# Copying the output/denominator bank of a sliding-window attention out of PSUM before the softmax is normalised

## The chip, the cores and the metric

The kernel runs on one core of one Trainium2 chip. The metric is device time in microseconds (us). The engines are PE (matmul; PEld is its weight load), DVE (VectorE), ACT (ScalarE), POOL (GpSimd) and SP (which issues DMAs).

## The reference

Two layers. Each is a sliding-window attention with a residual, then an MLP over the token axis with a residual, on x of shape 1 x 2048 x 512.

```python
def _A_ref(x, wqkv, wo):                      # 32 heads of 16, window of 256 tokens
    qkv = ((x @ wqkv).reshape(B, S, 3, H, Dh)).transpose(2, 0, 3, 1, 4)
    scores = einsum("bhqd,bhkd->bhqk", q, k) * Dh ** -0.5     # masked to 0 <= i - j < 256
    o = einsum("bhqk,bhkd->bhqd", softmax(scores), v)
    return o.transpose(0, 2, 1, 3).reshape(B, S, D) @ wo
def _B_ref(x, w1, b1, w2, b2):                # mixes tokens: w1 is 2048 x 1792, w2 1792 x 2048
    u = gelu(einsum("bsd,sf->bdf", layernorm(x), w1) + b1)
    return (einsum("bdf,fs->bds", u, w2) + b2).transpose(0, 2, 1)
# ... twice: x = x + A(layernorm(x)); x = x + B(layernorm(x))
```

## The kernel before

The kernel describes its work as operations with reads, writes and a cost in nanoseconds. A list scheduler in the kernel gives every operation a time, and with it a fixed place in its engine's queue; the chip then follows that order with semaphores. The scheduler also hands out buffers: an operation whose buffer is not free yet is placed later. So a scarce buffer shows in the order of an engine, not only in waits.

This kernel's matmuls write PSUM, of which it allots eight banks (`PS`, 128 x 8 x 512 in fp32); SBUF is its working memory. Three pairs of banks hold scores. The other two are one pool, shared by "od" (at most one bank: output and denominators of a head group, columns 0-255 and 256-511) and "f", the fillers: QKV, output projection and MLP matmuls that fit between the attention's matmuls.

```python
NPT = 6
pt = sb("pt", [P, NPT, 4, 512])                    # exp buffers, in bf16; w2 blocks borrow them too
rl = sb("rl", [P, 2, 2, 256], dt.float32)
psum2 = Pool("psum2", 3)                           # three pairs of banks for scores
psum = Pool("psum", 2)
psum.classes = {"od": [0, 1], "f": [0, 2]}         # [in use, at most]
# ... attention, for one head group o: 8 heads on 4 x 32 partitions, 256 tokens (64 groups over both layers)
prev_sc[0] = op("tensor", f_sc, ...)               # L614: scores into two pairs of banks
op("scalar", ... ACTF.Exp ...)                     # L628: exp of 128x1024 into pt, two for each set of scores
op("vector", f_mask, ...)                          # L638, L640: mask multiply in pt
op("tensor", f_pv, ... writes=[od[o]] ...)         # L654: p @ v and p @ ones into the od bank
# ... after the last PV of the group:
t, tr = od[o], Tile(p_rl)
op("scalar", lambda e: e.activation(rl[:, tr.slot, 0, :], bank(t)[:, 256:512], ACTF.Ln), ...)        # L671
op("scalar", lambda e: e.activation(rl[:, tr.slot, 1, :], rl[:, tr.slot, 0, :], ACTF.Exp, scale=-1.0), ...)  # L673
op("vector", lambda e: e.tensor_tensor(oT[:, to.slot, o, :], bank(t)[:, 0:256], rl[:, tr.slot, 1, :],
                                       op=ALU.mult), reads=[t, (tr, 1)], ...)                        # L676
```

The od bank is free again when L676 has read it: after an ln, an exp and a product on two engines. The MLP's first product is cut in two. Its first half (L738 before, L740 after the change) needs only the first eight token tiles, so it may fill gaps late in the attention. Its second half (L752, later L754) starts when the attention has ended. L778 (later L780) is the MLP's second product, and L685 (later L687) the output projection.

The softmax here doesn't subtract the row's maximum and nothing guards it: scores larger than these inputs give would overflow.

Of the kernel before, what the change touches and what calls it, by code (L numbers as in the profile page):

```python
# [6 lines left out]
dt = mybir.dt  # L7
ALU = mybir.AluOpType
ACTF = mybir.ActivationFunctionType

P = 128
# [282 lines left out]
def dve_cost(n, mult=1.0, psum=False, ptrs=0):  # L294
    return ((62 if psum else 66) + n * mult) / 0.96 + 60 * ptrs


def act_cost(n, ptrs=0, psum=True):
    return ((61 if psum else 112) + n) / 1.2 + 93 * ptrs
# [29 lines left out]
def bass_interleave_layers__sliding_block__mixer_token_mlp__prompt_kernel(  # L329
# [16 lines left out]
    NFT = F // P  # L346
    EPS = 1e-5
    SMSCALE = 0.25
    NPT = 6

    es = ExitStack()
    with es:
        sb = lambda name, shape, d=dt.bfloat16: es.enter_context(nc.sbuf_tensor(name, shape, d))
# [7 lines left out]
        kbd = sb("kbd", [P, 3, 4, 8, 2, 64])  # L361
        vbd = sb("vbd", [P, 3, 8, 16, 32])
        pt = sb("pt", [P, NPT, 4, 512])
        rl = sb("rl", [P, 2, 2, 256], dt.float32)
        oT = sb("oT", [P, 3, 4, 256])
        uT = sb("uT", [P, NFT, 512])
        w1b = sb("w1b", [P, 4, NT // 2, 256])
# [17 lines left out]
        op = g.op  # L385
# [4 lines left out]
        psum = Pool("psum", 2)  # L390
        psum.classes = {"od": [0, 1], "f": [0, 2]}
        p_xhT, p_qT, p_stg = Pool("xhT", 2), Pool("qT", 2), Pool("stg", 6)
        p_kv, p_pt, p_rl, p_oT = Pool("kv", 3), Pool("pt", NPT), Pool("rl", 2), Pool("oT", 3)
        p_w1 = Pool("w1", 4)


# [18 lines left out]
        def load_w(i):  # L415
# [9 lines left out]
           cost=2600, prio=-1e6)  # L425
# [3 lines left out]
           cost=500, prio=-1e6)  # L429
        op("sync", lambda e: dma_nc(e, bst[:, NFT:], B_b2.rearrange("(t p) -> p t", p=P)), writes=["b2s"], dma=True,  # L430
           cost=500, prio=-1e6)
# [4 lines left out]
        for h in range(2):  # L436
# [5 lines left out]
               reads=["ident"], writes=[("half", h)])  # L442
# [8 lines left out]
           reads=["tri"] + HALF, writes=["ld0"])  # L451
        op("vector", lambda e: e.scalar_tensor_tensor(ldm[:, 0, :], tri[:, 64:128], half[:, 1:2], ldm[:, 0, :],
                                                      op0=ALU.mult, op1=ALU.add), reads=["tri", "ld0"] + HALF,
           writes=["ld0"])
# [27 lines left out]
        def bank(t):  # L482
            return PS[:, 2 * t.slot if t.pool is psum2 else 6 + t.slot, :]
# [107 lines left out]
        def attention(c, tqs, tks):  # L591
            tq, qc = tqs[c // 2], 4 * (c % 2)
            blk = lambda j: (tks[(4 * c + j) // 8], (4 * c + j) % 8)
            plan = attention_plan(c == 0)
            nb = len(plan)
            half = plan[-1][2] * 64
            to = Tile(p_oT)
            for o2 in range(0, 4, 2):

                order = [[(k, o2, 0)] for k in range(nb - 1)] + [[(nb - 1, o2, 0), (nb - 1, o2 + 1, half)]] + \  # L600
                        [[(k, o2 + 1, 0)] for k in range(nb - 1)]
                od = {}
                left = {o2: nb, o2 + 1: nb}
                for su in order:
                    tp, tA, tB = Tile(p_pt), Tile(psum2), Tile(psum2)
                    cols = max(base + plan[k][2] * 64 for k, _, base in su)

                    def f_sc(e, su=su, tt=(tA, tB)):
                        last = None
                        for k, o, base in su:  # L610
                            for j, q0, n, c0 in plan[k][0]:
                                tk, jj = blk(j)
                                for r in range(4):
                                    last = e.matmul(  # L614
                                        PS[:, 2 * tt[r // 2].slot + r % 2, base + c0 * 64:base + (c0 + n) * 64],
                                        lhsT=kbd[32 * r:32 * r + 32, tk.slot, o, jj, :, :].rearrange("p h n -> p (h n)"),
                                        rhs=qT[32 * r:32 * r + 32, tq.slot, o, (qc + q0) * 64:(qc + q0 + n) * 64],
                                        start=True, stop=True, tile_position=(32 * r, 0), skip_group_check=True)
                        return last
                    rd = []  # L620
                    for k, o, _ in su:
                        rd.append((tq, o))
                        for tk in {id(blk(j)[0]): blk(j)[0] for j, _, _, _ in plan[k][0]}.values():
                            rd += [(tk, "k", o, h) for h in range(2)]
                    prev_sc[0] = op("tensor", f_sc, reads=rd, writes=[tA, tB], cost=cols / 2.4 + 15,
                                    prio=len(g.ops), after=[prev_sc[0]] if prev_sc[0] else [], cfg="sc", cls="sc")
                    for i, ts in enumerate((tA, tB)):
                        op("scalar", lambda e, ts=ts, tp=tp, i=i, cols=cols: e.activation(  # L628
                            pt[:, tp.slot, 2 * i:2 * i + 2, 0:cols], PS[:, 2 * ts.slot:2 * ts.slot + 2, 0:cols],
                            ACTF.Exp, scale=SMSCALE), reads=[ts, "acttab"], writes=[(tp, i)], cost=act_cost(2 * cols))  # L630
                    keys = [(tp, 0), (tp, 1)]
                    n = len(su)
                    for c0, nc_, w0 in plan[su[0][0]][1]:
                        def f_mask(e, tp=tp, n=n, c0=c0, w=nc_ * 64, w0=w0):
                            v = pt[:, tp.slot, :, c0 * 64:c0 * 64 + w]
                            msk = ldm[:].rearrange("p a b -> p (a b)")[:, w0 * 64:w0 * 64 + w]
                            if n == 1:
                                return e.tensor_tensor(v, v, msk.unsqueeze(1).to_broadcast([P, 4, w]), op=ALU.mult)  # L638
                            v = stepped(v, n, half)
                            return e.tensor_tensor(v, v, msk.unsqueeze(1).unsqueeze(1).to_broadcast([P, 4, n, w]),  # L640
                                                   op=ALU.mult)
                        op("vector", f_mask, reads=keys + LD, writes=keys, cost=dve_cost(4 * n * nc_ * 64, 0.5))
                    for k, o, base in su:
                        first = o not in od
                        if first:
                            od[o] = Tile(psum, 1, "od")

                        def f_pv(e, k=k, o=o, base=base, tp=tp, first=first, t=od[o]):
                            last, st = None, first
                            for j, q0, n, c0 in plan[k][0]:  # L650
                                tk, jj = blk(j)
                                for den in (0, 1):
                                    for r in range(4):
                                        last = e.matmul(  # L654
                                            bank(t)[32 * r:32 * r + 32, den * 256 + q0 * 64:den * 256 + (q0 + n) * 64],
                                            lhsT=onesbd[:] if den else vbd[:, tk.slot, jj, 4 * o + r, :],
                                            rhs=pt[:, tp.slot, r, base + c0 * 64:base + (c0 + n) * 64],
                                            start=st, stop=True, tile_position=(0, 32 * r), skip_group_check=True)
                                    st = False
                            return last  # L660
                        rd = ["ones"]
                        for j, _, _, _ in plan[k][0]:
                            tk, jj = blk(j)
                            rd += [(tk, "v", jj, h) for h in range(2)]
                        op("tensor", f_pv, reads=keys + rd, writes=[od[o]], cost=plan[k][2] * 128 / 2.4 + 15,
                           holds=[to], prio=len(g.ops), cfg="pv", cls="pv")
                        left[o] -= 1
                        if left[o]:
                            continue
                        t, tr = od[o], Tile(p_rl)  # L670
                        op("scalar", lambda e, t=t, tr=tr: e.activation(rl[:, tr.slot, 0, :], bank(t)[:, 256:512], ACTF.Ln),  # L671
                           reads=[t, "acttab"], writes=[(tr, 0)], cost=act_cost(256), prio=-1e5)
                        op("scalar", lambda e, tr=tr: e.activation(rl[:, tr.slot, 1, :], rl[:, tr.slot, 0, :], ACTF.Exp,  # L673
                                                                   scale=-1.0),
                           reads=[(tr, 0), "acttab"], writes=[(tr, 1)], cost=act_cost(256, psum=False), prio=-1e5)
                        op("vector", lambda e, t=t, tr=tr, o=o: e.tensor_tensor(  # L676
                            oT[:, to.slot, o, :], bank(t)[:, 0:256], rl[:, tr.slot, 1, :], op=ALU.mult),
                           reads=[t, (tr, 1)], writes=[(to, o)], cost=dve_cost(256, psum=True), prio=-1e5)
            return to

        def wo_block(c, to, wide):
# [171 lines left out]
```

## Time and profile before

The time is 527.25 us (median of three runs, 526.81 to 527.71). These lines are of the page of the profile: the span, busy time by engine, and busy tenths of PE and ACT in 40 slices of the span; then the shares of the chain of work that ended last.

```profile
span 525.3 us, 16776 instructions
...
PE 455.1 (87%) x7495; PEld 234.0 (45%) x7584; DVE 340.0 (65%) x715; ACT 340.1 (65%) x464; POOL 150.7 (29%) x266
...
PE   4977788878888899999988888999787889998997
...
ACT  0589999999999703403996997079999960231000
...
PE 46%; ACT 34%; DVE 16%; issue 1%; DMA 1%; POOL 1%
...
```

ACT is full in slices 4 to 13 and PE is full just after: the limit passes from ACT to PE and back. The chain that ended last says the same: 46% of the span is PE's, 34% ACT's. The next view gives busy time in stretches that I chose by what runs in them: attention of layer one, its MLP to the first L778, the way into layer two's attention, that attention in three parts, and the rest. Each line has start:end, length, then busy time (and instructions) of each engine.

```profile
...
core 0: us, PE busy (x) PEld busy (x) DVE busy (x) ACT busy (x) POOL busy (x), PEclk, DMA share, GB/s
45.00:181.00 136.00, 110.63 (x2842) 60.87 (x2870) 100.73 (x216) 132.59 (x181) 44.16 (x72) 1.00 0.14 37
181.00:220.50 39.50, 39.26 (x180) 17.89 (x183) 17.17 (x30) 10.06 (x15) 1.49 (x4) 1.00 0.64 174
220.50:254.00 33.50, 31.37 (x294) 15.54 (x300) 24.18 (x49) 10.99 (x15) 15.02 (x26) 1.00 0.12 32
254.00:300.00 46.00, 40.06 (x901) 22.10 (x902) 33.97 (x71) 41.70 (x58) 16.62 (x26) 1.00 0.13 32
300.00:342.00 42.00, 38.33 (x639) 19.70 (x644) 32.02 (x74) 24.56 (x35) 13.23 (x29) 1.00 0.48 108
342.00:429.00 87.00, 73.42 (x1741) 39.22 (x1760) 61.36 (x130) 82.87 (x110) 28.32 (x44) 1.00 0.10 27
429.00:525.30 96.30, 90.64 (x420) 40.83 (x420) 31.61 (x49) 11.42 (x17) 1.49 (x4) 1.00 0.47 137
...
```

In the first stretch ACT is busy 132.6 of 136 us and DVE 100.7, while PE is busy 110.6. In the second PE is busy 39.3 of 39.5 us. A caution: the profile of before has 7495 of 7584 matmul records, so PE's busy time is understated. All 7584 weight loads are in it, so I count work by those.

What ties the od bank up is seen in the timeline of a few microseconds (start, length, engine, line, operation; in brackets the idle time just before, and what ended it).

```profile
...
154.52 0.42 DVE L676 TENSOR_TENSOR oT<-PS,rl 128x256 bf16<-128x256 f32 x1
...
155.21 0.29 PE L654 MATMUL PS<-pt,vbd 128*32 128x256 bf16 x4
...
156.28 0.23 PE L654 MATMUL PS<-pt,onesbd 128*32 128x128 bf16 x4
...
157.08 0.69 DVE L742 COPY uT<-PS 128x512 f32<-128x512 f32 x1 [0.88 <-PE PS L738]
157.24 0.61 ACT L671 ACTIVATE rl<-PS 128x256 f32<-128x256 f32 x1
...
157.83 1.04 PE L738 MATMUL PS<-xh_sb,w1b 128*128 128x512 bf16 x4 [0.46 <-DVE uT L742]
158.41 0.66 ACT L673 ACTIVATE rl<-rl 128x256 f32<-128x256 f32 x1
...
159.09 0.42 DVE L676 TENSOR_TENSOR oT<-PS,rl 128x256 bf16<-128x256 f32 x1 [0.66 <-ACT rl L673]
...
159.69 0.21 PE L654 MATMUL PS<-pt,vbd 128*32 128x64 bf16 x4
...
```

The last PV matmuls start at 156.28. The ln starts at 157.24, the exp at 158.41, as each takes its turn among the long exps of ACT (L628, 128x1024: 1.09 us each in the mean). The product ends at 159.51, and only then may the next group's PV start, at 159.69. The product before it ended at 154.94 and PV followed at 155.21, so the bank was free for some 0.3 us between two groups. The fillers thus had the other bank alone: the copy L742 empties it from 157.08 to 157.77, and the next group of eight L738 matmuls begins only then, at 157.83. Taken over all groups of this attention in the trace, the bank is occupied 96% of the time, and the median from the end of the last PV to the product's end is 2.9 us. The view of waits has PE's share of this (us in total, times, longest):

```profile
...
PEld PS L654 <- DVE oT L676: 10.9, 22, 0.8
...
```

The last thing to read is how much of L738 was left after the attention. These are weight loads of L738 after the first attention and after the second (start:end, length, PEld busy and count, one for each matmul; then clock, DMA share, GB/s).

```profile
...
181.00:215.00 34.00, 6.04 (x62) 1.00 0.74 201
429.00:500.00 71.00, 7.36 (x76) 1.00 0.47 133
...
```

A matmul of this shape takes 0.217 us, so 62 and 76 of them are 13.5 and 16.5 us of PE time, run when PE is the only full engine.

### The profile page before, as it was taken

The page shows a single profiled execution, that of the slowest core. Times are in us where ns is not written, and L with a number is a line of the kernel's source. Part 1 is how long each engine was busy: PE and PEld are TensorE (multiplying, and loading weights), DVE is VectorE, ACT ScalarE, POOL GpSimd, SP SyncE. Part 2 cuts the span into 40 slices and gives each one's busy share as a digit, 9 for nine tenths or more (in the row PEclk, how much of TensorE's full clock was granted, in tenths as well). Part 3 has the DMA queues.
Part 4 walks back from the last instruction along what each step waited for, and adds up shares of the span by engine and source line. Part 5 has one row for each costly group of instructions (what it writes and reads, how often), then busy time and mean ns, then how long its engine had stood idle before and what let it go on. Part 6 is the DMA issues. An engine that isn't in the chain of part 4 may idle for free.

```text
span 525.3 us, 16776 instructions
## 1 busy us (share of the span) xinstructions
PE 455.1 (87%) x7495; PEld 234.0 (45%) x7584; DVE 340.0 (65%) x715; ACT 340.1 (65%) x464; POOL 150.7 (29%) x266
## 2 busy tenths in 40 slices
PE   4977788878888899999988888999787889998997
PEld 2543444444444444444454445445444444443443
DVE  6999687786785653377677876875778755332222
ACT  0589999999999703403996997079999960231000
POOL 3886234343420110027234411661533101000000
PEclk9989999999999999999999999999999999999999
DMA  8421100600002585310030008610000167453163
GB/s 272 70 43 23 32 14 3 162 2 2 2 3 84 146 226 159 93 50 10 12 94 2 3 12 200 133 23 12 12 2 2 43 178 206 126 137 98 41 194 105
DMA packets 81688, 39.89 MB, mean 76 GB/s; under 512 B 18128, under 2 KB 81616, under 8 KB 81616
## 3 DMA queue, kind: packets, MB, share of 16 engines
q1 hardware_dynamic: 81616, 38.81, 28.0%
q8 instruction: 59, 0.97, 0.8%
q14 instruction: 13, 0.11, 0.1%
HBM read 33.56 MB, written 2.10 MB: 68 GB/s over the span
## 4 chain that ended last, share of the span: by engine, by line
PE 46%; ACT 34%; DVE 16%; issue 1%; DMA 1%; POOL 1%
ACT pt L628 30%; PE PS L778 16%; PE PS L752 9%; PE PS L738 7%; PE PS L654 5%; PE PS L533 3%; DVE stats L462 3%; PE PS L558 2%; DVE pt L638 2%; ACT rl L671 2%; PE PS L614 2%; DVE xh_sb L475 2%; DVE stg L567 2%; ACT rl L673 2%; PE PS L685 2%
## 5 line engine op out<-in xcount | busy, mean ns | idle before, releaser
L628 ACT ACTIVATE pt<-PS 128x1024 bf16<-128x1024 f32 (+1 forms) x304 | 297.9, 1075 | 60.3 <-PE PS L614 58.7
L638 DVE TENSOR_TENSOR pt<-pt,ldm 128x512 bf16<-128x512 bf16 (+1 forms) x192 | 78.3, 408 | 38.3 <-ACT pt L628 37.0
L654 PE MATMUL PS<-pt,vbd 128*32 128x64 bf16 (+3 forms) x1920 | 80.6, 235 | 13.5 <-DVE stg L541 5.1
L654 PE MATMUL PS<-pt,onesbd 128*32 128x64 bf16 (+3 forms) x1920 | 78.6, 233 | 0.0
L533 PE MATMUL PS<-xhT,wqkv 128*128 128x512 bf16 x225 | 60.6, 390 | 14.0 <-DVE stg L541 3.5
L471 POOL TENSOR_SCALAR rstd<-agg 128x1 f32<-128x1 f32 x64 | 14.4, 226 | 193.8 <-DVE agg L464 192.5
L778 PE MATMUL PS<-uT,w2b 128*128 128x512 bf16 x263 | 61.6, 379 | 3.5 <-issue 2.1
L768 ACT ACTIVATE uT<-rl,b1col 128x512 bf16<-128x512 f32 x28 | 18.7, 714 | 70.0 <-DVE rl L762 70.0
L614 PE MATMUL PS<-qT,kbd 32*128 32x64 bf16 (+3 forms) x1920 | 60.8, 232 | 3.4 <-ACT pt L628 2.5
L654 PEld LDWEIGHTS PS<-pt,vbd 128*32 128x32 bf16 x1920 | 44.5, 96 | 42.9 <-DVE oT L676 10.9
L544 POOL TENSOR_SCALAR kbd<-stg,par 128x512 bf16<-128x512 bf16 x64 | 49.7, 786 | 47.8 <-DVE stg L541 46.9
L570 POOL TENSOR_SCALAR vbd<-stg,half 128x512 bf16<-128x512 bf16 x64 | 48.6, 771 | 38.7 <-DVE stg L567 37.9
L738 PE MATMUL PS<-xh_sb,w1b 128*128 128x512 bf16 x209 | 50.1, 380 | 7.0 <-DVE w2b L742 2.4
L614 PEld LDWEIGHTS PS<-qT,kbd 32*128 32x128 bf16 x1920 | 27.8, 93 | 53.5 <-ACT pt L628 31.8
L783 DVE SCALAR_TENSOR_TENSOR x_sb<-PS,b2col,x_sb 128x512 bf16<-128x512 f32 x32 | 23.9, 750 | 39.3 <-PE PS L778 39.2
L752 PE MATMUL PS<-xh_sb,w1b 128*128 128x512 bf16 x220 | 48.5, 379 | 0.2
L654 PEld LDWEIGHTS PS<-pt,onesbd 128*32 128x32 bf16 x1920 | 45.7, 97 | 0.2
L462 DVE BATCH_NORM_STATS2 stats<-x_sb 128x6 f32<-128x512 bf16 x64 | 43.5, 685 | 0.6
L558 PE MATMUL PS<-wqkv,xhT 128*64 128x256 bf16 x512 | 36.3, 281 | 5.1 <-DVE stg L567 1.8
L778 PE MATMUL PS<-uT,pt 128*128 128x512 bf16 x162 | 37.5, 379 | 2.6 <-DVE rl L762 1.5
L778 PEld LDWEIGHTS PS<-uT,w2b 128*128 128x128 bf16 x280 | 25.4, 98 | 32.0 <-DVE x_sb L688 0.9
L685 PE MATMUL PS<-wo_sb,oT 128*128 128x512 bf16 x112 | 30.5, 381 | 10.5 <-DVE x_sb L688 5.1
(44 smaller groups left out, 451.0 us busy)
## 6 DMA issues: line engine op xcount, KB each, us to landing
w1b<-in_B_w_dram SPq DMA_DIRECT2D x28, 512.0 KB, 4.2
w2b<-in_B_w_dram SPq DMA_DIRECT2D x10, 896.0 KB, 5.3
pt<-in_B_w_dram SPq DMA_DIRECT2D x12, 448.0 KB, 6.4
out_dram<-x_sb SPq DMA_DIRECT2D x16, 128.0 KB, 1.7
wqkv<-in_A_wqkv_dram SPq DMA_DIRECT2D x3, 512.0 KB, 7.2
x_sb<-in_A_x_dram SPq DMA_DIRECT2D x3, 512.0 KB, 8.8
x_sb<-in_A_x_dram SPq DMA_DIRECT2D x2, 256.0 KB, 2.7
wo_sb<-in_A_wo_dram SPq DMA_DIRECT2D x1, 512.0 KB, 10.0
```

Source lines behind the costliest of these rows:

```text
L462: op("vector", lambda e: e.bn_stats(stats[:, t, :], x_sb[:, t, :]), reads=[f"x{t}"], writes=[f"st{t}"], cost=dve_cost(512))
L533: mm_group(ft, 4, lambda e, c: e.matmul(bank(ft), lhsT=wqkv[:, c, which * 512 + o * P:which * 512 + (o + 1) * P], rhs=xhT[:, tx.slot, c, : ...
L544: op("gpsimd", lambda e, h=h: e.tensor_scalar(kbd[:, tk.slot, o, :, h, :], stg[:, ts.slot, :].rearrange("p (s n) -> p s n", n=64), par[:, ...
L558: last = e.matmul(bank(ft)[64 * hf:64 * hf + 64, sc * 256:(sc + 1) * 256], lhsT=xhT[:, tx.slot, c, tok:tok + 64], rhs=wqkv[:, c, 1024:1536 ...
L570: op("gpsimd", lambda e, h=h: e.tensor_scalar(vbd[:, tk.slot, 2 * sp:2 * sp + 2, :, 16 * h:16 * h + 16], stg[:, ts.slot, :].rearrange("p ( ...
L614: last = e.matmul(PS[:, 2 * tt[r // 2].slot + r % 2, base + c0 * 64:base + (c0 + n) * 64], lhsT=kbd[32 * r:32 * r + 32, tk.slot, o, jj, :, ...
L628: op("scalar", lambda e, ts=ts, tp=tp, i=i, cols=cols: e.activation(pt[:, tp.slot, 2 * i:2 * i + 2, 0:cols], PS[:, 2 * ts.slot:2 * ts.slot ...
L638: return e.tensor_tensor(v, v, msk.unsqueeze(1).to_broadcast([P, 4, w]), op=ALU.mult)
L654: last = e.matmul(bank(t)[32 * r:32 * r + 32, den * 256 + q0 * 64:den * 256 + (q0 + n) * 64], lhsT=onesbd[:] if den else vbd[:, tk.slot, j ...
L738: mm_group(ft, 8, lambda e, sc, tt=tt, ft=ft: e.matmul(bank(ft), lhsT=w1b[:, tw.slot, sc, tt * P:(tt + 1) * P], rhs=xh_sb[:, sc, :], start ...
L752: last = e.matmul(PS[:, 2 * tu.slot + tt, :], lhsT=w1b[:, tw.slot, sc - 8, tt * P:(tt + 1) * P], rhs=xh_sb[:, sc, :], start=(sc == 8), sto ...
L778: mm_group(ft, NFT, lambda e, fc: e.matmul(bank(ft), lhsT=w(fc)[:, k * P:(k + 1) * P], rhs=uT[:, fc, :], start=(fc == 0), stop=(fc == NFT ...
```

## The change

Its intent is to free the od bank sooner. One DVE operation copies the whole bank to SBUF, and the rest works on the copy: ln and exp in place, the product on POOL. Four copies may be alive, where rl had two slots; the two more take as much SBUF as one exp buffer, so there are five of those. (The MLP's second half keeps its sums in rl too, so it also gets four slots for two.) The reason is in the trace before: the bank is held for 2.9 us (median) after the last PV of a group.

```diff
-    NPT = 6
+    NPT = 5
-        rl = sb("rl", [P, 2, 2, 256], dt.float32)
+        rl = sb("rl", [P, 4, 2, 256], dt.float32)
 # ... and Pool("rl", 2) becomes Pool("rl", 4)
                         t, tr = od[o], Tile(p_rl)
-                        op("scalar", ... e.activation(rl[:, tr.slot, 0, :], bank(t)[:, 256:512], ACTF.Ln), ...)
-                        op("scalar", ... e.activation(rl[:, tr.slot, 1, :], rl[:, tr.slot, 0, :], ACTF.Exp, scale=-1.0), ...)
-                        op("vector", ... e.tensor_tensor(oT[:, to.slot, o, :], bank(t)[:, 0:256], rl[:, tr.slot, 1, :],
-                           op=ALU.mult), reads=[t, (tr, 1)], writes=[(to, o)], cost=dve_cost(256, psum=True), prio=-1e5)
+                        op("vector", ... e.tensor_copy(rl[:, tr.slot].rearrange("p a b -> p (a b)"), bank(t)),
+                           reads=[t], writes=[tr], cost=dve_cost(512, psum=True), prio=-1e5)
+                        op("scalar", ... e.activation(rl[:, tr.slot, 1, :], rl[:, tr.slot, 1, :], ACTF.Ln), ...)
+                        op("scalar", ... e.activation(rl[:, tr.slot, 1, :], rl[:, tr.slot, 1, :], ACTF.Exp, scale=-1.0), ...)
+                        op("gpsimd", ... e.tensor_tensor(oT[:, to.slot, o, :], rl[:, tr.slot, 0, :], rl[:, tr.slot, 1, :],
+                           op=ALU.mult), reads=[tr], writes=[(to, o)], cost=750)
```

More of the change, by code (lines that the diff above doesn't have):

```diff
@@ L392, in bass_interleave_layers__sliding_block__mixer_token_mlp__prompt_kernel @@
         p_xhT, p_qT, p_stg = Pool("xhT", 2), Pool("qT", 2), Pool("stg", 6)
-        p_kv, p_pt, p_rl, p_oT = Pool("kv", 3), Pool("pt", NPT), Pool("rl", 2), Pool("oT", 3)
+        p_kv, p_pt, p_rl, p_oT = Pool("kv", 3), Pool("pt", NPT), Pool("rl", 4), Pool("oT", 3)
         p_w1 = Pool("w1", 4)
@@ L670, in attention @@
                         t, tr = od[o], Tile(p_rl)
-                        op("scalar", lambda e, t=t, tr=tr: e.activation(rl[:, tr.slot, 0, :], bank(t)[:, 256:512], ACTF.Ln),
-                           reads=[t, "acttab"], writes=[(tr, 0)], cost=act_cost(256), prio=-1e5)
-                        op("scalar", lambda e, tr=tr: e.activation(rl[:, tr.slot, 1, :], rl[:, tr.slot, 0, :], ACTF.Exp,
-                                                                   scale=-1.0),
-                           reads=[(tr, 0), "acttab"], writes=[(tr, 1)], cost=act_cost(256, psum=False), prio=-1e5)
-                        op("vector", lambda e, t=t, tr=tr, o=o: e.tensor_tensor(
-                            oT[:, to.slot, o, :], bank(t)[:, 0:256], rl[:, tr.slot, 1, :], op=ALU.mult),
-                           reads=[t, (tr, 1)], writes=[(to, o)], cost=dve_cost(256, psum=True), prio=-1e5)
+                        op("vector", lambda e, t=t, tr=tr: e.tensor_copy(
+                            rl[:, tr.slot].rearrange("p a b -> p (a b)"), bank(t)), reads=[t], writes=[tr],
+                           cost=dve_cost(512, psum=True), prio=-1e5)
+                        op("scalar", lambda e, tr=tr: e.activation(rl[:, tr.slot, 1, :], rl[:, tr.slot, 1, :], ACTF.Ln),
+                           reads=[tr, "acttab"], writes=[tr], cost=act_cost(256, psum=False), prio=-1e5)
+                        op("scalar", lambda e, tr=tr: e.activation(rl[:, tr.slot, 1, :], rl[:, tr.slot, 1, :], ACTF.Exp, scale=-1.0),
+                           reads=[tr, "acttab"], writes=[tr], cost=act_cost(256, psum=False), prio=-1e5)
+                        op("gpsimd", lambda e, tr=tr, o=o: e.tensor_tensor(
+                            oT[:, to.slot, o, :], rl[:, tr.slot, 0, :], rl[:, tr.slot, 1, :], op=ALU.mult),
+                           reads=[tr], writes=[(to, o)], cost=750)
             return to
```

## The prediction

> **What bounds the kernel now.** By the chain of waits, PE makes up 46% of the span, ACT 34%, DVE 16%. By busy time per stretch: from 45 to 179 us (first attention layer) ACT is busy 132.6 of 134 us, PE 109 (25 us idle), DVE 99.6. From 179 to 232 us PE is busy 98%. The second layer repeats this: 254-300 us ACT 91%, 300-342 us PE 91% with ACT idle 17 us, 342-430 us ACT 95% with PE idle 14 us, then PE 96% to the end.
> So PE idles while ACT is full and ACT idles while PE is full. The timeline shows why the work is not spread better: about 14.5 us of first-MLP matmuls (L738) per layer run after the attention (184-197 and 432-447 us), although their inputs were there earlier. These matmuls, QKV and output projection fill PE's gaps through one PSUM bank, the other of that pair being the output/denominator bank. That bank is held all the time: PV matmuls 155.2-156.4 us, then ln (157.2), exp (158.4), product (159.1-159.5), next PV at 159.7. A filler group of 1.75 us takes some 4.5 us.
>
> **What the change does, per head group (64 of them).**
> - The bank is released by a DVE copy of 128x512 fp32 from PSUM (0.69 us, as the same-shaped L742 copy) about 1 us after the last PV, instead of some 3 us. Released earlier, it serves as a second filler bank perhaps 30-45% of the time.
> - DVE: +0.69 -0.42 = +0.27 us, 17 us in all; the ACT-bound stretches go from about 74% DVE to 83-88%, with the fillers' evictions that move in.
> - ACT: ln reads SBUF instead of PSUM. In the chain a PSUM ln adds 0.28 us, an SBUF exp 0.30, so +0.02 us, 1.3 us in all.
> - GpSimd: +64 products of 256 fp32. [...] the mask multiply L638 takes 0.41 us, but 0.70 us at 96.7 us, under a GpSimd operation. I allow some 8 us of DVE, spread out.
> - Five exp buffers instead of six: a buffer's life gets shorter as PV waits less for the bank, so five should do in layer one. In layer two three instead of four are left until the third w2 block is used (about 257 us); up to 1 us lost.
>
> **On the critical path.** In the ACT-bound stretches nothing is gained directly (+0.6 us). The gain is PE work pulled into PE's 25 us (layer one) and 20 us (layer two) of idle time: I expect about 6 to 8 us per layer, as PE then runs near 90%, against 2 us of losses. The start (16-45 us, DVE 98% busy) loses 1 us.
>
> **Prediction: 514.5 us, 504 to 525.** Faster by over 2%: 0.55; within 2%: 0.39; slower: 0.06.
>
> **Right if:** L738 starts well before 149.8 us and at most 9 us of it run after the attention; PE busy in 122-179 us reaches 90%; waits of PE for the product are gone; ACT stays above 97% from 45 us to the end of attention; DVE busy rises by 17-28 us. The 300-342 us stretch gets shorter.
>
> **Wrong if:** DVE becomes the limit, so that copies, masks and evictions queue and ACT's ln waits for copies; if five exp buffers make scores wait; or if fillers are limited by dependencies, not by the bank (then within 1%).

The sum came to a gain of 12.7 us (527.25 us before, 514.5 forecast): 6 to 8 us of PE work moved in each of two layers, less the losses; how the terms make 12.7 was not written out. Some are cut where marked: the time of one product on GpSimd, the load of all 64, where they would be on the critical path and what that would cost (one of the losses), and the reason given for longer mask multiplies. No trace before the change shows that product, and the reason was not shown. The 8 us of DVE are my guess from one multiply (0.70 us under the GpSimd operation L570, for 0.41) and no term of the 12.7 us.

## The result, and the profile after

The time is 505.49 us (median of four runs, 504.15 to 505.92), before 527.09 us beside it. The ratio is 0.9584, with a 95% interval of 0.9564 to 0.9604. Ratios in this document are the mean time of one kernel's fast runs over that of the other's in the same rounds, so not quite the ratio of the medians quoted.

The same lines of the page, after:

```profile
span 503.9 us, 16930 instructions
...
PE 471.2 (94%) x7584; PEld 231.2 (46%) x7584; DVE 357.8 (71%) x715; ACT 342.6 (68%) x464; POOL 202.0 (40%) x330
...
PE   3977989999999999999999999999989899999997
...
ACT  1597999999999964404993999399979980330000
...
PE 45%; ACT 31%; DVE 18%; POOL 4%; issue 1%; DMA 1%
...
```

PE is at 9 tenths in nearly all slices from the seventh on. (Of the rise from 455.1 to 471.2 us most is lost records, see above; what really changed is the idle time, from about 56 to 33 us. The chain's shares hardly moved: both engines still bound it, in a shorter span.) DVE is 17.8 us busier, POOL 51, ACT 2.5. The same stretches, with the same columns, cut at the same events:

```profile
...
45.00:183.00 138.00, 132.03 (x2908) 66.79 (x2912) 114.73 (x231) 135.30 (x182) 70.26 (x106) 1.00 0.20 50
183.00:208.50 25.50, 24.72 (x136) 10.97 (x125) 12.17 (x22) 9.90 (x15) 2.69 (x6) 1.00 0.73 187
208.50:242.00 33.50, 32.36 (x315) 15.86 (x313) 24.36 (x50) 11.32 (x16) 14.21 (x26) 1.00 0.17 46
242.00:288.00 46.00, 43.47 (x825) 21.59 (x822) 36.65 (x72) 37.28 (x52) 24.22 (x39) 1.00 0.14 34
288.00:328.00 40.00, 38.75 (x719) 19.03 (x718) 33.43 (x68) 32.40 (x45) 21.53 (x36) 1.00 0.46 114
328.00:413.50 85.50, 80.87 (x1760) 40.11 (x1760) 69.00 (x137) 80.83 (x107) 36.53 (x58) 1.00 0.10 26
413.50:503.90 90.40, 87.22 (x404) 39.19 (x402) 30.54 (x47) 11.45 (x17) 2.22 (x6) 1.00 0.51 146
...
```

Now PE and ACT are both full in the first stretch: 132.0 and 135.3 of 138 us. It is 2 us longer; the second is 14.0 us shorter (25.5 for 39.5). The way into layer two takes 33.5 us, as before. Layer two's attention takes 171.5 us for 175.0, and the rest 90.4 for 96.3. These differences (both tables begin at 45 us) add up to the 21.4 us between the spans.

The timeline over the same part of the attention:

```profile
...
150.44 0.21 PE L654 MATMUL PS<-pt,vbd 128*32 128x64 bf16 x4
...
152.92 0.23 PE L654 MATMUL PS<-pt,onesbd 128*32 128x128 bf16 x4
...
153.63 0.67 DVE L671 COPY rl<-PS 128x512 f32<-128x512 f32 x1
...
154.58 1.90 PE L740 MATMUL PS<-xh_sb,w1b 128*128 128x512 bf16 x8
...
154.80 0.60 ACT L674 ACTIVATE rl<-rl 128x256 f32<-128x256 f32 x1
...
155.80 0.68 DVE L744 COPY uT<-PS 128x512 f32<-128x512 f32 x1
156.01 0.61 ACT L676 ACTIVATE rl<-rl 128x256 f32<-128x256 f32 x1
...
156.70 0.74 POOL L678 TENSOR_TENSOR oT<-rl 128x256 bf16<-128x256 f32 x1 [0.73 <-ACT rl L676]
...
156.74 0.29 PE L654 MATMUL PS<-pt,vbd 128*32 128x256 bf16 x4
...
```

The group's PV starts at 150.44, the last at 152.92; the copy ends at 154.30 and the bank is free. Ln, exp and product go on until 157.44, off the bank. At 154.58 eight L740 matmuls run without a break: four end one filler group and four begin the next, before the copy L744 (155.80) has emptied the bank of the first. That takes two filler banks. The next group's PV (156.74) starts before this group's product has ended. Over all groups of this attention the bank is occupied 77% of the time (96% before), and the median from the end of the last PV to the release is 1.0 us (2.9 before). In layer two it is 67% (80% before). The wait of 10.9 us has shrunk to 2.0 us; a new one appears, of the output projection for POOL's product (2.4 us of it at the start of the first attention, the rest at the ends of both):

```profile
...
PEld PS L687 <- POOL oT L678: 2.9, 3, 2.4
...
PEld PS L654 <- DVE rl L671: 2.0, 6, 0.7
...
```

And the weight loads of the MLP's first half that are left after the attentions, as above:

```profile
...
183.00:215.00 32.00, 0.00 (x0) 1.00 0.69 181
413.50:500.00 86.50, 5.60 (x58) 1.00 0.53 151
...
```

The first L740 runs at 121.1 us, where the first L738 ran at 149.8. After the first attention none of the 62 is left; after the second 58 of 76 are.

### The profile page after: what moved, and what is told of

Its sections match the earlier page's. It is cut to its first block, busy times and chain, and to the rows that moved or that the text cites. A ratio compares the mean times of both kernels' runs of the same rounds, so it can differ in the third digit from the quotient of the medians.

```text
span 503.9 us, 16930 instructions
## 1 busy us (share of the span) xinstructions
PE 471.2 (94%) x7584; PEld 231.2 (46%) x7584; DVE 357.8 (71%) x715; ACT 342.6 (68%) x464; POOL 202.0 (40%) x330
## 4 chain that ended last, share of the span: by engine, by line
PE 45%; ACT 31%; DVE 18%; POOL 4%; issue 1%; DMA 1%
ACT pt L628 27%; PE PS L780 16%; PE PS L754 10%; PE PS L740 5%; PE PS L654 5%; DVE pt L638 3%; PE PS L533 3%; PE PS L614 3%; DVE stats L462 3%; PE PS L687 2%; DVE xh_sb L475 2%; ACT rl L674 2%; DVE stg L567 2%; ACT rl L676 2%; DVE qT L538 2%; DVE rl L671 1%
## 5 line engine op out<-in xcount | busy, mean ns | idle before, releaser
L654 PE MATMUL PS<-pt,vbd 128*32 128x64 bf16 (+3 forms) x1920 | 82.8, 237 | 7.1 <-DVE pt L638 4.7
L678 POOL TENSOR_TENSOR oT<-rl 128x256 bf16<-128x256 f32 x64 | 48.1, 751 | 91.7 <-ACT rl L676 91.1
L654 PE MATMUL PS<-pt,onesbd 128*32 128x64 bf16 (+3 forms) x1920 | 81.8, 233 | 0.0
L533 PE MATMUL PS<-xhT,wqkv 128*128 128x512 bf16 x256 | 67.0, 392 | 2.8 <-DVE stg L541 0.9
L780 PE MATMUL PS<-uT,w2b 128*128 128x512 bf16 x280 | 65.8, 380 | 0.8 <-DVE rl L671 0.8
L544 POOL TENSOR_SCALAR kbd<-stg,par 128x512 bf16<-128x512 bf16 x64 | 51.2, 811 | 27.6 <-DVE stg L541 23.8
L740 PE MATMUL PS<-xh_sb,w1b 128*128 128x512 bf16 x224 | 55.1, 381 | 1.7 <-DVE w2b L744 0.8
L570 POOL TENSOR_SCALAR vbd<-stg,half 128x512 bf16<-128x512 bf16 x64 | 50.4, 799 | 13.1 <-DVE stg L567 8.4
L614 PEld LDWEIGHTS PS<-qT,kbd 32*128 32x128 bf16 x1920 | 27.6, 93 | 57.5 <-ACT pt L628 37.6
L754 PE MATMUL PS<-xh_sb,w1b 128*128 128x512 bf16 x224 | 49.2, 379 | 0.8 <-DVE x_sb L690 0.8
L671 DVE COPY rl<-PS 128x512 f32<-128x512 f32 x64 | 43.6, 681 | 2.9 <-PE PS L654 2.3
L473 POOL TENSOR_TENSOR rstd<-rstd,mhalf 128x1 f32<-128x1 f32 x64 | 39.0, 610 | 3.8
L475 DVE TENSOR_SCALAR xh_sb<-x_sb,agg,rstd 128x512 bf16<-128x512 bf16 x64 | 32.9, 515 | 10.4 <-POOL rstd L473 9.6
```

The source lines that it names most:

```text
L533: mm_group(ft, 4, lambda e, c: e.matmul(bank(ft), lhsT=wqkv[:, c, which * 512 + o * P:which * 512 + (o + 1) * P], rhs=xhT[:, tx.slot, c, : ...
L544: op("gpsimd", lambda e, h=h: e.tensor_scalar(kbd[:, tk.slot, o, :, h, :], stg[:, ts.slot, :].rearrange("p (s n) -> p s n", n=64), par[:, ...
L570: op("gpsimd", lambda e, h=h: e.tensor_scalar(vbd[:, tk.slot, 2 * sp:2 * sp + 2, :, 16 * h:16 * h + 16], stg[:, ts.slot, :].rearrange("p ( ...
L614: last = e.matmul(PS[:, 2 * tt[r // 2].slot + r % 2, base + c0 * 64:base + (c0 + n) * 64], lhsT=kbd[32 * r:32 * r + 32, tk.slot, o, jj, :, ...
L654: last = e.matmul(bank(t)[32 * r:32 * r + 32, den * 256 + q0 * 64:den * 256 + (q0 + n) * 64], lhsT=onesbd[:] if den else vbd[:, tk.slot, j ...
L671: op("vector", lambda e, t=t, tr=tr: e.tensor_copy(rl[:, tr.slot].rearrange("p a b -> p (a b)"), bank(t)), reads=[t], writes=[tr], cost=dv ...
```

## The experiments

Theory A: the gain is the bank given back early, so that PE work which stood after the attention fills PE's idle time in it. It has two parts: fillers get a second bank (A1), and the next group's PV can start earlier (A2). Rival B: what counts is the product's move from DVE to POOL. Rival C: what counts is a lucky order. The scheduler fixes all queues, and any change of a number reorders them, so each run below has its own order beside its edit. (That rl has four slots is no rival by itself: e1 and e5 have them too.)

All eleven runs gave correct results, with three rounds each against the kernel before (527.2 to 527.5 us in those rounds).

| run | what | us | ratio to before |
|---|---|---|---|
| the change | | 505.49 | 0.9584 |
| e1_hold_exp | bank held to the end of exp | 533.09 | 1.0108 |
| e5_hold_ln | bank held to the end of ln | 525.07 | 0.9956 |
| e2_after_f1 | change, one filler bank | 513.58 | 0.9730 |
| e11_after_f1_order2 | the same, other order | 514.48 | 0.9756 |
| e3_before_f1 | before, one filler bank | 526.18 | 0.9977 |
| e4_prod_dve | change, product on DVE | 513.48 | 0.9735 |
| e10_prod_dve_order2 | the same, other order | 507.49 | 0.9624 |
| e6_six_buffers | change, six exp buffers | 505.27 | 0.9578 |
| e7_cost780 | change, other order | 511.34 | 0.9695 |
| e8_tuned | change, best order found | 503.23 | 0.9542 |
| e9_before_order2 | before, best order found | 521.38 | 0.9886 |

### Holding the bank longer

For e1, against the changed kernel (`holds=[t]` keeps the bank until that operation has ended; no data changes):

```diff
-  op("scalar", ... ACTF.Exp, scale=-1.0), reads=[tr, "acttab"], writes=[tr], cost=...)
+  op("scalar", ... ACTF.Exp, scale=-1.0), reads=[tr, "acttab"], writes=[tr], holds=[t], cost=...)
```

> The changed kernel, but the output/denominator bank is given back only when the exp of its denominators has ended, not when the DVE copy has; the copy, the ACT work, the GpSimd product and the five buffers stay. Theory A (the gain is the early return of the bank): most of the gain goes, 518 to 530 us, and 10 us or more of L740 stands after the first attention again. Theory B (the gain is that the product left DVE's queue or that GpSimd took it): stays within 3 us of 505.5 us.

It took 533.09 us, 3 us beyond A's range and far from B's. All other parts of the change are in it, and it is 1.1% slower than the kernel before. The weight loads of L740 after its attentions, in the view used above:

```profile
...
183.50:215.00 31.50, 4.21 (x44) 1.00 0.62 174
434.50:500.00 65.50, 7.27 (x76) 1.00 0.50 142
...
```

So 44 of them are back after the first attention (six more ran even later; 10.9 us in all), and 76 after the second. The bank was occupied 94% of the time in layer one. The timed difference to the change, 27.6 us, is more than the whole gain. Why e1 is slower than the kernel before is not shown: it pays for the copy without its use, it has five exp buffers for six, and its order differs. (e1 with six buffers was not run.)

e5 moves the same `holds=[t]` to the ln.

> The changed kernel, but the bank is given back when the ln has ended, one ACT step later than the copy and one earlier than in e1 (533.1 us). If the time follows how long the bank is held: between the two, 512 to 524 us. If only the exp's end mattered (an order effect of e1): within 3 us of 505.5 us.

It took 525.07 us, a microsecond above the range. The weight loads of L740 after its attentions:

```profile
...
185.20:215.00 29.80, 3.58 (x38) 1.00 0.68 188
432.00:500.00 68.00, 5.54 (x58) 1.00 0.52 145
...
```

So 38 are back after the first attention; after the second there are 58, as with the change, and layer one carries most of the loss: the first PV weight load of layer two starts at 251.0 us here and at 236.2 with the change. Release after copy, ln and exp gives 505.5, 525.1 and 533.1 us. The time goes up with the hold, but not in proportion: the median from the last PV to the release is 1.0, 1.7 and 2.9 us, while layer one's bank is occupied 77%, 94% and 94% of the time. (These are my counts over the traces. For e5 no view here shows them; what one shows is that PE waited 6.8 us in layer one for the ln before a PV.) The first step, the shorter one, already takes most of the bank's free time, and most of the gain with it. The 8 us from e5 to e1 are no more than two orders of one kernel differ by (e7 and e8, below). Reading the denominators straight from PSUM by ACT would keep the bank for an ACT operation too (the ln from PSUM, L671 before, took 0.44 us in the mean, and waited its turn). I wrote such a version (ln from PSUM, DVE copying the output half only), but the kernel's scheduler found no order for it, with five buffers or six, so it is untried. The same happened to the change with the bank held until the product, and to the kernel before with five exp buffers: fillers then occupy both banks while they wait for a weight block that waits for an exp buffer. Five buffers were thus not possible without the change, as the scheduler stands.

### How many filler banks

```diff
-        psum.classes = {"od": [0, 1], "f": [0, 2]}
+        psum.classes = {"od": [0, 1], "f": [0, 1]}
```

> The changed kernel, but filler matmuls may hold one PSUM bank of the pair at most (before and after: two). Splits theory A. A1 (the gain is the second filler bank): 520 to 528 us. A2 (the gain is that the next head group's PV can start earlier, so that exp buffers and PE order loosen up): below 508 us. Both: in between, 509 to 519 us.

> The kernel before with the same cap of one filler bank. If the output/denominator bank was held nearly always there, as the timeline between 152 and 166 us showed, fillers had in effect one bank already: within 1% of 527 us (522 to 532). If fillers did use the second bank often, 535 us or more.

The cap costs the changed kernel 8 us (513.58) and the kernel before nothing (526.18, 0.2% faster, less than order alone can do). So before, fillers had one bank in effect; the change gave them a second for part of the time. The 13 us from 527 to 514 remain without it. PV that starts earlier (A2) is the candidate for them, but the rest of the change and its order are in them too. The trace of e2 fits A2: PE's wait for the bank before a PV is 3.3 us in all (10.9 before), and 36 and 40 weight loads of L740 are left after its attentions (62 and 76 before), although fillers had one bank. To see how much of the 8 us was order, I gave the capped kernel another one.

> The cap of one filler bank, as in e2 (513.6 us), in another order (2500 ns, 185 ns), the first of which alone the changed kernel has. If the second filler bank is worth 5 us or more beyond order luck, 509 us or more; if e2 was mostly order, 503 to 508 us.

It took 514.48 us: the cap costs 3 to 11 us against the three orders of the uncapped kernel that ran (503.2, 505.5, 511.3), and 7 us by the means of both.

### The product's engine

```diff
-                        op("gpsimd", lambda e, tr=tr, o=o: e.tensor_tensor(
+                        op("vector", lambda e, tr=tr, o=o: e.tensor_tensor(
 # and cost=dve_cost(256), prio=-1e5 for cost=750
```

> The changed kernel with the product on DVE again, now from the copy (128x256 fp32 from SBUF, some 0.42 us, 64 of them: +27 us of DVE, -48 us of GpSimd). Theory A: most of the gain stays, as the bank still comes back early, but DVE at 90% in the attention delays copies and evictions: 508 to 517 us. Theory B (GpSimd taking the product is what counts): 520 us or more.

> The product on DVE, as in e4 (513.5 us), in another order (3000 ns, 215 ns). If the 8 us of e4 were DVE's load (27 us more of it), this stays at 510 us or more; if they were mostly order, it comes to 503 to 508 us, and the move to GpSimd is worth little.

The 0.42 us in the first of these is the time of L676 before, which read the bank (417 ns in the mean). That the product takes as long on DVE from SBUF, and so the 27 us of both texts, is an estimate from that; no view here shows it.

e4 took 513.48 us, e10 507.49. The second has the product on DVE and keeps 3.8% of the 4.2%. Rival B, which asked for 520 us or more, falls. What the move to POOL is worth lies within the spread of orders: 8 us between the first orders, 4 us between the best that I ran of both (507.5 and 503.2).

### Exp buffers

The edit is `NPT = 6` for 5; the SBUF has room for it.

> The changed kernel with six exp buffers as before and four copies. If five buffers cost something (prediction: up to 1 us in layer two), 503 to 505.5 us. If five are enough: within 1% of 505.5 us either way, since any change of the order moves the time by some us.

It took 505.27 us, 0.2 us less than the change. Both of my ranges hold that, so a cost of five buffers is not seen, but up to 1 us of it could hide under the order. Its page is the one used above to weigh lost records:

```profile
span 504.2 us, 16833 instructions
...
PE 455.9 (90%) x7487; PEld 231.1 (46%) x7584; DVE 357.2 (71%) x715; ACT 342.6 (68%) x464; POOL 203.1 (40%) x330
...
```

### Order alone

e7 changes one number, which no instruction sees:

```diff
-                           reads=[tr], writes=[(to, o)], cost=750)
+                           reads=[tr], writes=[(to, o)], cost=780)
```

> The changed kernel with nothing changed but the number the kernel's own scheduler takes for the product, 780 ns for 750 (the chip took 729 ns). No operation changes, only their static order. Rival theory C (a good part of the 21 us is a lucky order): 510 us or more. Theory A: within 1.3% of 505.5 us, 503 to 512.

It took 511.34 us. My two ranges overlapped there, so by itself it settles nothing between A and C, but it shows the size of luck: 5.9 us, 1.2%, from the same instructions in another order. The profile has the place: 22 of the L740 weight loads (4.8 us) are after 183 us now, and the first L780 starts at 213.7 us, where it did at 208.3.

```profile
...
183.00:215.00 32.00, 2.16 (x22) 1.00 0.58 160
419.00:500.00 81.00, 5.69 (x60) 1.00 0.57 157
...
```

So I asked what order alone can do for the kernel before. In e9 the scheduler lets a ready PV overtake fillers after 3000 ns, for 2500, and assumes 185 ns from a matmul to its consumer, for 205.

> The kernel before with the two scheduler numbers moved (PV precedence after 3000 ns, matmul latency 185 ns): the same operations in the best order that I found for it. It asks how much the order alone gives the kernel before. Theory A with some order luck: 519 to 526 us. Theory C (the change is mainly a luckier order): 512 us or less.

It took 521.38 us: 5.8 us from order, but not 21. Rival C accounts for a part only. The same two numbers for the change (3500 and 185) make e8.

> The changed kernel with two numbers of its scheduler changed: a ready PV matmul is given precedence over fillers after 3500 ns, not 2500, and the assumed matmul-to-consumer latency is 185 ns, not 205. No operation changes. With the bank no longer scarce PV may wait longer, so fillers fill better: 500 to 505 us; if PE, 94% busy, leaves nothing: 504 to 508.

It took 503.23 us and is the fastest version. Its ratio to before, 0.9542 (0.9528 to 0.9556), lies just below that of the change. In the best order that I found for each, the kernels stand at 521.4 and 503.2 us, 3.5% apart; as given, 4.2%. I searched only a few dozen orders of each, by the scheduler's own plan and not by time, so this is no bound.

## Why the prediction was right, and where its sizes were off

The measured 505.49 us lie in the range of 504 to 525, and "faster by over 2%" (given 0.55) was right. The forecast gain of 12.7 us was 21.6. Point by point:

- **The mechanism** was right: a scarce bank, not an engine, kept first-MLP matmuls out of the attention. e1 and e5 show it: they undo only the early release, and lose 27.6 and 19.6 us, where orders of one kernel differed by up to 8 us (e7 and e8).
- **The time that the bank is free** was guessed at 30-45%. It is 23% in layer one and 33% in layer two. The gain is nevertheless larger than forecast, and e2 leaves 13 us of it with no second filler bank at all. The prediction counted only the filler bank as a source of gain; PV starting earlier is what it left out, though how much that gave is not shown.
- **The step that was mis-sized** is "I expect about 6 to 8 us per layer, as PE then runs near 90%". From the first stretch to the first L780 the gain is 12.0 us in layer one, and 9.4 us after it. PE reached 96% of the first stretch, and 98.6% of 122-179 us (83% before, with lost records), where 90% were expected. In layer one all 62 waiting matmuls moved, where I allowed some to stay. "At most 9 us of it run after the attention" held there and failed in layer two: 58 loads, 12.6 us.
- **Part of the excess may be order**: e7 has the same instructions and gains 16 us, nearer to the forecast. The prediction had no term for this, either way, and how near 505.49 fell to the lower end of its range (1.5 us) is luck: with e7's order it would have been 511.
- **PE's idle time** of 25 us in layer one was read from a trace with lost records. By weight loads and 0.16 us for each lost record, it was some 21 us in that stretch, and 6 us are left. The direction of the argument did not depend on it.
- **DVE** rose by 17.8 us, as costed (17 us of it the copy: 64 of 681 ns for 64 of 417). The extra 8 us for mask multiplies under POOL operations did not come: their mean went from 408 to 401 ns, with 48 us of products added on POOL. Only 11 of the 192 started while a product ran; five of these took 0.76 to 0.92 us, where those that no POOL operation touched took 0.42 us (128x512) or 0.29 us (128x256) in the mean (all after the change).
- **ACT** rose 2.5 us (1.3 costed). In its full queue the chain of waits advanced by 0.27 to 0.28 us for an ln from PSUM (before, 120-160 us) and by 0.30 to 0.31 us for one from SBUF (after, 118-165 us). "ACT stays above 97% from 45 us to the end of attention" held in layer one (133.5 of 135.8 us). Layer two, which the prediction had at 91% at its start, went down (37.3 of 46 us in its first part, 41.7 before), while PE was busy 43.5 us of it. "The 300-342 us stretch gets shorter" held: 40 us for 42.
- **POOL**: the product takes 729 ns in the median, 751 in the mean, 48.1 us in all.
- **The waits for the product** went, as said, except for 2.9 us before output projections.

What stays open is how the 21 us divide between a second filler bank, earlier PV and order. The cap costs 7 us by the means, 13 us remain under it, and order moves either kernel by some 6 us; the first two were only told apart by the cap, whose own order differs.

## What to carry to other kernels

When one engine is full in one stage and another in the next, look for work of the second that could have run in the first, and for the buffer that kept it out: here one PSUM bank that stood occupied for 2.9 us after its last matmul, while ln and exp took their turns in a full queue (ACT busy 132.6 of 136 us). A copy that does no arithmetic can pay, if it takes a scarce bank off a chain through a full engine: 64 copies of 0.68 us and the rest of the change made DVE, which was not full (busy 340.0 of 525.3 us, and 100.7 of 136 in the first attention), 17.8 us busier, and the kernel 21.6 us faster. In a statically ordered kernel, run a change in two or three orders before believing its last per cent: one number that changes no instruction moved this one by 1.2%.
